# Attention followed by two gated MLPs on one core: the second batch's query side is issued between the first gate products

## Chip, cores and metric

One NeuronCore of a Trainium2 chip runs the whole program. The metric is the device time of one execution in microseconds (us). The kernel before took 1736.15 us (median of 3 runs, 1733.27 to 1736.31).

## What is computed

Eight batches of eight heads, 576 positions, head width 64. A pack of 32 queries per head first attends to keys and values; the queries `q` then attend to the 32 packed rows. The result, 4608 tokens of 512 values, is scaled by its root mean square and goes through a gated MLP (512 to 1536 to 512, SiLU) and a second one (512 to 2048 to 512).

```python
p_packed = sm_attn(p, k, v)                 # softmax over 576 keys
out      = sm_attn(q, p_packed, p_packed)   # softmax over 32 packed rows
x   = out as (4608, 512)
xn  = x / sqrt(mean(x*x) + 1e-6) * rms_g
h   = (silu(xn @ w_gate) * (xn @ w_val)) @ w_out
u   = h @ w_in
res = (u * sigmoid(1.702 * u)) @ w_out2
```

## The kernel before

**Chains.** `attention` (L121) works on chains: chain n is one half of a batch's heads (four heads; NG = 2 halves per batch, so chains 0 and 1 are batch 0, chains 2 and 3 batch 1). Two batches make a unit; there are four units. A chain has two sides.

- The packed side: load k, p, v (L156), transposes of k and p on TensorE (`heads_t` L263 and `p_t` L247), first scores `s1` (L274 on TensorE, maxima L284 to L289 on VectorE, exponentials L293 on ScalarE), transposes of the exponentials `a_t` (L307), product with v `pv` (L319), transposes of that `pp_t` (L340), which also writes the weights' left side `Lh`, `Ll` (L349 to L351).
- The query side: load q (`load_q`), ten transposes `heads_t(n, "q", ...)` (L263), second scores `s2` (two groups of columns, 256 and 320; L274), then in a row: transposes to `t` on VectorE (L359), maxima (L364), subtraction on GpSimd (L365), exponentials on ScalarE (L366), sums (L368 to L371), multiplication on GpSimd (L372), `weights`, a transpose into the tile `AT` on VectorE (L378), products `x` (L396) whose squares are summed on ScalarE (L401, tile `jk`). When both halves of a batch are squared, the mean square and its power follow (L408, L409 on VectorE, L411 on GpSimd) and `scale` (L414) multiplies `AT` by it (matmul L422, product L431). `scaled` (L634) then splits `AT` into `Aqh` and `Aql` (L642, L643), which the gate products read.

**The first MLP.** `run` (in `mlp1`) goes through steps; step s is 128 columns of the gate and value weights. `prods` (L610) makes the step's stationary tiles `Wh`, `Wl` (matmul L628, L630, L631). `gateval(s, o)` (L644, matmul L659, o the batch within the unit) makes gate and value; `project` (L679) multiplies by `w_out`. The weights arrive as packed words and are converted piece by piece: `piece` (L573) runs `convert` (L102: ScalarE L108, VectorE L109 to L112, ScalarE L113, GpSimd L114) and then fetches the next raw piece (L570) into one of two `raw` buffers, so that a fetch waits for the conversion of the piece two before.

**What sets the order.** For unit 0 `start` (L433) writes a list of calls, each with a number (a position, not a measured time), sorted by it. Calls below LEADING = 38 are issued first, with conversions between them (L982 to L987). The rest is given out while `run` issues the first gate products: one call per EVERY/len(todo) estimated TensorE ns (L992, L1018). When `run` yields "attention" (after step 1 of batch 0), all that is left is issued, then `scaled(0, 1)` and the gate products of batch 1. A scheduler at build time then settles each engine's order; the engines run their instructions in that order. The query tiles and, from chain 4 on, the key tiles share one tag `kq` with two buffers in pool `at`; all loads go through the SP queue.

```python
while todo[0][0] < LEADING:
    time, calls = todo.pop(0)
    act(calls)
    while time > spent:
        piece()
        spent += PACE
```

Of the kernel before, what the change touches and what calls it, by code (L numbers as in the profile page):

```python
# [28 lines left out]
def tile_pack_attention__then__two_mlps(  # L29
# [32 lines left out]
    NG = H * NP // P  # L62
# [56 lines left out]
    chains = [(b, g) for b in range(B) for g in range(NG)]  # L119

    def attention(at, first, lp, psum, getL, getAT):  # L121
# [311 lines left out]
        def start(period, after):  # L433


            todo = []

            def do(time, *calls):
                todo.append((time, len(todo), calls))

            for n in range(LEAD):
                t0 = period * n
                do(t0 - 50 if n < 2 else t0 - 2 * period + 2.6, (load_kp, n))
                do(t0 - 30 if n < 1 else t0 - period + 2.5, (load_v, n))
                do(t0 - 29 if n < 1 else t0 - period + (3.5, 14)[n > 1], (load_q, n))
                do(t0 + 1.2, (p_mask, n), (p_t, n))
                for i in range(4):
                    do(t0 + 0.5 * i, (heads_t, n, "k", i // 2, i % 2))
                do(t0 + 3.5, (s1, n, 0))
                do(t0 + 4.2, (s1, n, 1))  # L450
                do(t0 + 3.0, (split_v, n))
                do(t0 + 8, (a_t, n, 0))
                do(t0 + 8.6, (a_t, n, 1))
                do(t0 + 11, (pv, n))
                do(t0 + 14.5, (pp_t, n))
                for i in range(4):
                    do(t0 + 11.2 + 0.5 * i, (heads_t, n, "q", i // 2, i % 2))
                do(t0 + 17, (s2, n, 0))
                do(t0 + 17.7, (s2, n, 1))
                do(t0 + 23, (weights, n))  # L460
                for i in range(-(-NC // 2)):
                    do(t0 + 25 + 0.6 * i, (x, n, 2 * i))
                if n % NG == NG - 1:
                    for e in range(2):
                        do(t0 + 30 + 0.6 * e, (scale, chains[n][0], e))
            t0 = period * LEAD
            do(t0 + 2, (load_kp, after))
            do(t0 + 14, (load_v, after))
            do(t0 + 15, (load_q, after))
            do(t0 + 20, (p_mask, after), (p_t, after))  # L470
            for i in range(4):
                do(t0 + 23.1 + 0.5 * i, (heads_t, after, "k", i // 2, i % 2))
            return [(t, calls) for t, _, calls in sorted(todo, key=lambda x: x[:2])]

        def stages(seq, after, whole):
# [52 lines left out]
            return todo  # L528

        return start, stages  # L530


# [541 lines left out]
```

## Time and profile before

| what | value |
|---|---|
| runs | 1733.27, 1736.31, 1736.15 us |
| profiled execution | 1733.05 us, its span 1731.3 us |
| TensorE matmul (PE) | 1690.9 us, 98% of the span |
| VectorE (DVE) | 896.6 us, 52% |
| ScalarE (ACT) | 683.1 us, 39% |
| GpSimd (POOL) | 497.1 us, 29% |
| granted TensorE clock, mean | 0.997 |

Busy times are means over stages with different limits: VectorE is busy for 88% of the stretch from 100 to 300 us, far more than over the whole span. A chain that decides something is read from the timeline of its engines, and a wait from the row of the instruction that waits.

### The profile page before, as it was taken

The page shows a single profiled execution, that of the slowest core. Times are in us where ns is not written, and L with a number is a line of the kernel's source. Part 1 is how long each engine was busy: PE and PEld are TensorE (multiplying, and loading weights), DVE is VectorE, ACT ScalarE, POOL GpSimd, SP SyncE. Part 2 cuts the span into 40 slices and gives each one's busy share as a digit, 9 for nine tenths or more (in the row PEclk, how much of TensorE's full clock was granted, in tenths as well). Part 3 has the DMA queues.
Part 4 walks back from the last instruction along what each step waited for, and adds up shares of the span by engine and source line. Part 5 has one row for each costly group of instructions (what it writes and reads, how often), then busy time and mean ns, then how long its engine had stood idle before and what let it go on. Part 6 is the DMA issues. An engine that isn't in the chain of part 4 may idle for free.

```text
span 1731.3 us, 24694 instructions
## 1 busy us (share of the span) xinstructions
PE 1690.9 (98%) x9400; PEld 1497.7 (87%) x9400; DVE 896.6 (52%) x1792; ACT 683.1 (39%) x1511; POOL 497.1 (29%) x479
## 2 busy tenths in 40 slices
PE   7899999999999999999999999999999999999998
PEld 5699898999999999999988888888888888888887
DVE  6888898557666576678884742222222222122221
ACT  5676676655555555555553321111111111111111
POOL 2446777544554354445643200000000000000000
PEclk9999999999999999999999999999999999999999
DMA  9556656544425442356656410101010101000000
GB/s 263 153 168 196 194 177 198 176 139 145 125 88 172 142 143 97 105 206 235 235 192 226 145 58 1 49 0 49 1 49 0 49 0 49 0 21 4 18 8 25
DMA packets 152343, 186.16 MB, mean 108 GB/s; under 512 B 87073, under 2 KB 123937, under 8 KB 145185
## 3 DMA queue, kind: packets, MB, share of 16 engines
q1 hardware_dynamic: 152224, 184.58, 33.4%
q8 instruction: 74, 1.21, 0.3%
q14 instruction: 45, 0.36, 0.1%
HBM read 139.46 MB, written 45.09 MB: 107 GB/s over the span
## 4 chain that ended last, share of the span: by engine, by line
PE 86%; DVE 5%; DMA 3%; ACT 3%; issue 1%; POOL 1%; SPq 1%; ACTq 0%; POOLq 0%; DVEq 0%
PE ps_dn L885 23%; PE ps_up L866 23%; PE ps_o L690 15%; PE ps_g L659 15%; PE ps_w L628 3%; PE ps_at L274 2%; PE ps_at L319 2%; PE ps_at L263 2%; PE ps_at L396 1%; DMA raw<-in_moe_w_in_dram 1%; DMA raw<-in_moe_w_out_dram 1%; DVE Wl L631 1%; DMA raw<-in_moe_w_val_dram 1%; SPq L156 1%; ACT Wh L630 1%
## 5 line engine op out<-in xcount | busy, mean ns | idle before, releaser
L866 PE MATMUL ps_up<-xh,wi 128*128 128x512 f32 x1152 | 381.8, 393 | 2.4 <-issue 1.6
L885 PE MATMUL ps_dn<-wo,gh 128*128 128x512 f32 x1152 | 356.4, 391 | 0.0
L690 PE MATMUL ps_o<-Hh,wo 128*128 128x384 f32 x1152 | 325.5, 341 | 4.2 <-ACT add L703 2.9
L872 DVE CAST gh<-gf 128x512 fp32r<-128x512 f32 x144 | 63.3, 440 | 509.0 <-ACT gf L869 508.9
L869 ACT ACTIVATE gf<-ps_up 128x512 f32<-128x512 f32 x144 | 86.2, 599 | 609.7 <-PE ps_up L866 588.6
L866 PEld LDWEIGHTS ps_up<-xh,wi 128*128 128x128 f32 x1152 | 216.2, 188 | 52.1 <-POOL wo L114 2.0
L885 PEld LDWEIGHTS ps_dn<-wo,gh 128*128 128x128 f32 x1152 | 216.3, 188 | 47.5
L659 PE MATMUL ps_g<-Aqh,Wh 128*128 128x288 f32 x768 | 235.4, 307 | 11.4 <-DVE th L667 4.1
L659 PE MATMUL ps_g<-Aqh,Wl 128*128 128x288 f32 x768 | 226.6, 296 | 0.6 <-DVE Wl L631 0.6
L659 PE MATMUL ps_g<-Aql,Wh 128*128 128x288 f32 x768 | 227.0, 296 | 0.0
L866 PE MATMUL ps_up<-xl,wi 128*128 128x512 f32 x576 | 225.8, 392 | 0.0
L885 PE MATMUL ps_dn<-wo,gl 128*128 128x512 f32 x576 | 224.4, 391 | 0.0
L690 PEld LDWEIGHTS ps_o<-Hh,wo 128*128 128x128 f32 x1152 | 209.9, 188 | 8.7 <-ACT add L703 4.0
L690 PE MATMUL ps_o<-Hl,wo 128*128 128x384 f32 x576 | 193.3, 337 | 0.8 <-POOL Hl L676 0.8
L676 POOL TENSOR_TENSOR Hl<-th,Hh 128x576 fp32r<-128x576 f32 x96 | 137.8, 1436 | 176.3 <-ACT Hh L675 174.3
L631 DVE TENSOR_TENSOR Wl<-ps_w,Wh 64x512 fp32r<-64x512 f32 x192 | 131.7, 687 | 80.6 <-ACT Wh L630 77.6
L659 PEld LDWEIGHTS ps_g<-Aqh,Wh 128*128 128x128 f32 x768 | 144.8, 189 | 17.7 <-DVE th L667 5.5
L705 POOL TENSOR_TENSOR acc<-acc,add 128x384 f32<-128x384 f32 x135 | 136.3, 1021 | 68.8 <-ACT add L703 67.0
L659 PEld LDWEIGHTS ps_g<-Aqh,Wl 128*128 128x128 f32 x768 | 144.5, 188 | 1.2 <-DVE Wl L631 0.8
L659 PEld LDWEIGHTS ps_g<-Aql,Wh 128*128 128x128 f32 x768 | 145.1, 189 | 0.0
L630 ACT CAST Wh<-ps_w 64x512 fp32r<-64x512 f32 x192 | 111.5, 581 | 79.1 <-PE ps_w L628 47.7
L885 PEld LDWEIGHTS ps_dn<-wo,gl 128*128 128x128 f32 x576 | 108.1, 188 | 24.7
(150 smaller groups left out, 2527.7 us busy)
## 6 DMA issues: line engine op xcount, KB each, us to landing
wg<-wg SPq DMA_DIRECT2D x48, 1024.0 KB, 5.4
wo<-wo SPq DMA_DIRECT2D x48, 512.0 KB, 4.1
raw<-in_moe_w_out_dram SPq DMA_DIRECT2D x28, 512.0 KB, 3.6
x<-acc SPq DMA_DIRECT2D x32, 288.0 KB, 2.7
out_dram<-ob SPq DMA_DIRECT2D x36, 256.0 KB, 2.0
vn<-in_v_dram SPq DMA_DIRECT2D x16, 512.0 KB, 6.3
qn<-in_q_dram SPq DMA_DIRECT2D x64, 128.0 KB, 5.0
raw<-in_moe_w_in_dram SPq DMA_DIRECT2D x16, 512.0 KB, 3.9
```

What stands on the lines that cost most here:

```text
L263: nc.tensor.transpose(ps[:, o : o + size(c)], src[: size(c), c, 2 * a : 2 * a + 2, :].rearrange("p h d -> p (h d)"), ident[: size(c), : si ...
L628: nc.tensor.matmul(ps[:, a], st[:, i], mv[:, i], start=n == 0, stop=n == 2)
L630: nc.scalar.copy(Wh[rows, :, g], src)
L631: nc.vector.tensor_sub(Wl[rows, :, g], src, fl(Wh[rows, :, g]))
L659: nc.tensor.matmul(ps, st[:, o, g, c * P : (c + 1) * P], mv[:, g, cols], start=n == 0, stop=n == 3 * NG - 1)
L676: nc.gpsimd.tensor_sub(Hl, th, fl(Hh))
L690: nc.tensor.matmul(ps, st[:, m * P : (m + 1) * P], mv[:, cols], start=n == 0, stop=n == 3 * len(ss) - 1)
L705: nc.gpsimd.tensor_add(a, a, t)
L866: nc.tensor.matmul(ps, st[:, i], mv[:, i], start=n == 0, stop=n == 3 * NM - 1)
L869: nc.scalar.activation(gf, ps, AF.Gelu_apprx_sigmoid)
L872: nc.vector.tensor_copy(gh, gf)
L885: nc.tensor.matmul(pacc[r], st[:, r * P : (r + 1) * P], mv, start=f == 0 and n == 0, stop=f == NF2 - 1 and n == 2,)
```

## The change

In `start`, the query side of chains 2 and 3 (batch 1 of unit 0: `heads_t` "q", `s2`, `weights`, `x`, `scale`) gets 24 added to its numbers, so that all of it lies above LEADING. It is issued in the second part of the list, between the first gate products. The calls for chain 4 (the next unit's first: `load_kp`, `load_v`, `load_q`, `p_mask`, `p_t`, `heads_t` "k") get new numbers too. The second part has 30 entries in place of 19.

```diff
             for n in range(LEAD):
                 t0 = period * n
+                late = 24 if n >= NG else 0
...
                 for i in range(4):
-                    do(t0 + 11.2 + 0.5 * i, (heads_t, n, "q", i // 2, i % 2))
-                do(t0 + 17, (s2, n, 0))
-                do(t0 + 17.7, (s2, n, 1))
-                do(t0 + 23, (weights, n))
+                    do(late + t0 + 11.2 + 0.5 * i, (heads_t, n, "q", i // 2, i % 2))
+                do(late + t0 + 17, (s2, n, 0))
+                do(late + t0 + 17.7, (s2, n, 1))
+                do(late + t0 + 23, (weights, n))
                 for i in range(-(-NC // 2)):
-                    do(t0 + 25 + 0.6 * i, (x, n, 2 * i))
+                    do(late + t0 + 25 + 0.6 * i, (x, n, 2 * i))
                 if n % NG == NG - 1:
                     for e in range(2):
-                        do(t0 + 30 + 0.6 * e, (scale, chains[n][0], e))
+                        do(late + t0 + 30 + 0.6 * e, (scale, chains[n][0], e))
             t0 = period * LEAD
-            do(t0 + 2, (load_kp, after))
-            do(t0 + 14, (load_v, after))
-            do(t0 + 15, (load_q, after))
-            do(t0 + 20, (p_mask, after), (p_t, after))
+            do(t0 + 24, (load_kp, after))
+            do(t0 + 25, (load_v, after))
+            do(t0 + 31, (load_q, after))
+            do(t0 + 32, (p_mask, after), (p_t, after))
             for i in range(4):
-                do(t0 + 23.1 + 0.5 * i, (heads_t, after, "k", i // 2, i % 2))
+                do(t0 + 34 + 0.5 * i, (heads_t, after, "k", i // 2, i % 2))
```

No instruction is added or removed. Lines below L443 are one higher in the changed kernel (L659 there is L660). Three places of the new order follow; `ps_at`, `ps_g` and `ps_w` are accumulator banks, the numbers behind names are tile numbers.

**Place 1.** TensorE at chain 3's first scores (`kTh_504`, `pTh_539`); `AT00` is chain 0's tile, `vn_287` chain 2's values. Before:

```order
L274 MATMUL ps_at_553<-qTh_453,kept_451 128x256 x2
L274 MATMUL ps_at_558<-kTh_504,pTh_539 128x256 x2
L274 MATMUL ps_at_612<-kTh_504,pTh_539 128x320 x2
L396 MATMUL ps_at_626<-pph_310,AT00_139 128x256 x2
L263 MATMUL ps_at_633<-ident_99,qn_486 128x128 x2
L263 MATMUL ps_at_633<-ident_99,qn_486 128x64
```

Now:

```order
L274 MATMUL ps_at_553<-qTh_453,kept_451 128x256 x2
L274 MATMUL ps_at_558<-kTh_504,pTh_539 128x256 x2
L396 MATMUL ps_at_621<-pph_310,AT00_139 128x256 x2
L396 MATMUL ps_at_628<-pph_310,AT00_139 64x256
L274 MATMUL ps_at_576<-qTh_453,kept_451 128x320 x2
L396 MATMUL ps_at_592<-pph_310,AT00_139 128x256 x2
L319 MATMUL ps_at_599<-vn_287,aTh_525 128x256 x5
L274 MATMUL ps_at_607<-kTh_504,pTh_539 128x320 x2
```

The second half of chain 3's first scores (128x320) moved behind chain 0's products, chain 1's second scores and chain 2's product with v.

**Place 2.** ScalarE around the last squares of batch 0 (`jk` with `ss_590`); `w<-raw` is the first step of a conversion, which needs a piece fetched from memory. Before:

```order
L401 ACTIVATE jk_744,ss_590<-ps_at_741 128x256
L135 COPY qTh_736<-ps_at_748 128x320
L401 ACTIVATE jk_746,ss_590<-ps_at_741 128x256
L135 COPY qTh_736<-ps_at_762 128x256
L113 CAST wg_771<-w_772 128x4x128
L135 COPY qTh_736<-ps_at_766 128x320
L135 COPY kept_734<-ps_at_783 128x256
L401 ACTIVATE jk_755,ss_590<-ps_at_753 64x256
```

Now:

```order
L113 CAST wo_660<-w_661 128x512
L113 CAST wg_716<-w_717 128x4x128
L108 ACTIVATE w_898<-raw_670 128x512
L401 ACTIVATE jk_692,ss_590<-ps_at_689 128x256
L108 ACTIVATE w_1053<-raw_726 128x512
L401 ACTIVATE jk_694,ss_590<-ps_at_689 128x256
L135 COPY kept_687<-ps_at_705 128x256
L401 ACTIVATE jk_698,ss_590<-ps_at_696 64x256
L643 CAST Aqh_786<-AT00_139 128x576
```

Two conversions' first steps moved in front of the last three squares of batch 0. On the SP queue the fetch of `raw_726` moved to the place right behind that of `raw_670`, ahead of chain 4's loads.

**Place 3.** TensorE ahead of batch 1's scale (`ri_1045` now, `ri_974` before); `AT10` and `AT11` are the tiles of chains 2 and 3, `Aqh_786` and `Aqh_853` batch 0's. Before, chain 3's second scores and its products stand among the first products of the MLP:

```order
L274 MATMUL ps_at_823<-qTh_736,kept_734 128x256 x2
L274 MATMUL ps_at_839<-qTh_736,kept_734 128x320 x2
L396 MATMUL ps_at_871<-kept_605,AT10_141 128x256 x2
L396 MATMUL ps_at_878<-kept_605,AT10_141 128x256 x2
L396 MATMUL ps_at_898<-kept_605,AT10_141 64x256
L422 MATMUL ps_at_794<-ident_99,ri_760 128x128 x2
L422 MATMUL ps_at_800<-ident_99,ri_760 128x128 x2
```

Now:

```order
L660 MATMUL ps_g_1064<-Aqh_786,Wl_820 128x288
L396 MATMUL ps_at_967<-kept_605,AT10_141 128x256 x2
L263 MATMUL ps_at_984<-ident_99,kn_802 128x128 x2
L263 MATMUL ps_at_989<-ident_99,kn_802 128x128 x2
L263 MATMUL ps_at_989<-ident_99,kn_802 128x64
L396 MATMUL ps_at_995<-kept_605,AT10_141 128x256 x2
L396 MATMUL ps_at_1010<-kept_605,AT10_141 64x256
L396 MATMUL ps_at_1015<-kept_687,AT11_142 128x256 x2
L396 MATMUL ps_at_1031<-kept_687,AT11_142 128x256 x2
L396 MATMUL ps_at_1038<-kept_687,AT11_142 64x256
L422 MATMUL ps_at_1047<-ident_99,ri_1045 128x128 x2
```

Chain 2's and chain 3's products moved from around batch 0's scale (`ri_760`) to a place behind the last gate product of batch 0 (`ps_g_1064`), directly ahead of batch 1's scale.

## Rows read from the trace of the kernel before

**Rows 1.** The page, part 1: busy time and share of the span.

```profile
PE 1690.9 (98%) x9400; PEld 1497.7 (87%) x9400; DVE 896.6 (52%) x1792; ACT 683.1 (39%) x1511; POOL 497.1 (29%) x479
```

**Rows 2.** Windows: stretch, length, busy us (instructions) of PE, PEld, DVE, ACT, POOL, clock, DMA.

```profile
42.80:91.76 48.96, 42.30 (x218) 31.92 (x217) 40.96 (x82) 31.82 (x94) 21.66 (x26) 0.97 0.53 158
100.00:300.00 200.00, 192.23 (x1302) 181.93 (x1301) 175.39 (x363) 139.90 (x325) 136.36 (x131) 1.00 0.62 190
```

**Rows 3.** Waits of PE, 42.8 to 91.8 us: total us, times, longest us.

```profile
PE ps_g L659 <- ACT Wh L630: 3.7, 2, 3.2
PE ps_at L274 <- ACT kept L135: 2.2, 2, 1.6
```

**Rows 4.** Timeline of PE: start us, us, engine, line, out<-in, xcount [idle before <-releaser].

```profile
41.75 2.14 PE L274 MATMUL ps_at<-kTh,pTh 128*128 128x256 f32 x8
43.73 1.03 PE L396 MATMUL ps_at<-pph,AT 128*128 128x256 f32 x4
...
47.15 2.52 PE L319 MATMUL ps_at<-vn,aTh 128*128 128x256 f32 x10
...
52.97 2.21 PE L274 MATMUL ps_at<-qTh,kept 128*128 128x256 f32 x8 [0.66 <-ACT kept L135]
...
60.14 1.43 PE L263 MATMUL ps_at<-ident,qn 128*128 128x128 f32 x8
...
63.50 2.21 PE L274 MATMUL ps_at<-qTh,kept 128*128 128x256 f32 x8 [1.56 <-ACT kept L135]
...
68.17 1.52 PE L422 MATMUL ps_at<-ident,ri 128*128 128x128 f32 x10
...
74.57 0.40 PE L659 MATMUL ps_g<-Aqh,Wh 128*128 128x288 f32 x1 [3.25 <-ACT Wh L630]
...
85.00 0.60 PE L422 MATMUL ps_at<-ident,ri 128*128 128x128 f32 x4
...
91.76 0.37 PE L659 MATMUL ps_g<-Aqh,Wh 128*128 128x288 f32 x1
...
96.02 0.29 PE L659 MATMUL ps_g<-Aqh,Wh 128*128 128x288 f32 x1
...
97.48 0.29 PE L659 MATMUL ps_g<-Aqh,Wl 128*128 128x288 f32 x1
```

**Rows 5.** Timeline of ACT (ScalarE), same columns.

```profile
46.86 0.48 ACT L293 ACTIVATE e<-ps_at,nm 128x256 f32<-128x256 f32 x1
...
59.49 0.70 ACT L108 ACTIVATE w<-raw 128x512 f32<-128x512 f32 x1 [2.34 <-DMA raw<-in_moe_w_val_dram]
...
63.29 0.39 ACT L401 ACTIVATE jk<-ps_at 64x256 f32<-64x256 f32 x1
...
80.74 0.38 ACT L401 ACTIVATE jk<-ps_at 64x256 f32<-64x256 f32 x1
```

**Rows 6.** Timeline of the SP queue: issue of transfers, same columns.

```profile
55.70 0.38 SPq L570 DMA_DIRECT2D raw<-in_moe_w_val_dram  x1
...
65.42 4.07 SPq L156 DMA_DIRECT2D qn<-in_q_dram  x5
```

**Rows 7.** Timelines of DVE (VectorE) and POOL (GpSimd), same columns.

```profile
53.35 0.69 DVE L111 SCALAR_TENSOR_TENSOR between<-raw,between 128x512 int32<-128x512 int32 x1
53.94 0.77 DVE L378 STREAM_TRANSPOSE AT<-t 128x576 f32<-128x576 f32 x1
...
64.79 0.77 DVE L378 STREAM_TRANSPOSE AT<-t 128x576 f32<-128x576 f32 x1
...
74.52 0.78 DVE L378 STREAM_TRANSPOSE AT<-t 128x576 f32<-128x576 f32 x1 [0.45 <-POOL t L372]
...
65.76 1.18 POOL L411 TENSOR_TENSOR ri<-ms,mhalf 128x5 f32<-128x5 f32 x1 [0.40 <-DVE ms L409]
...
83.50 1.17 POOL L411 TENSOR_TENSOR ri<-ms,mhalf 128x5 f32<-128x5 f32 x1
```

**Rows 8.** Windows, columns as in rows 2.

```profile
76.00:77.00 1.00, 1.00 (x5) 0.82 (x4) 0.97 (x3) 0.44 (x1) 0.00 (x0) 0.50 0.00 0
```

## The prediction, made before the changed kernel ran

> **What bounds the kernel now.** The page's first part comes first: TensorE is busy for 1690.9 us, 98% of the span [rows 1], so whatever this change gives or takes must show as TensorE waiting less or more; the work itself stays. The windows tell where waiting is left. From 42.8 us, where the two orders first differ on TensorE, to 91.76 us, where batch 1's first gate product starts, TensorE is busy 42.30 of 48.96 us, so it waits 6.7 us; from 100 to 300 us it waits another 7.8 (200 less 192.23) [rows 2]. The list of waits names the first stretch's: 3.7 us for `Wh` and 2.2 us for `kept`, both ScalarE's [rows 3]. The timelines then give the chain: chain 3's second scores end at 65.7 (63.50 and 2.21), batch 0's scale starts at 68.17, the first gate product at 74.57 after a wait of 3.25, batch 1's scale at 85.00, batch 1's first product at 91.76 [rows 4]. So before, the 26 us that chain 3 needs from its second scores to batch 1's first product lie beside other TensorE work.
>
> **What the change moves.** It adds and removes nothing. Behind batch 0's scale now stand, of batch 1's two chains, twenty transposes, both second scores and both products. The best it can bring is that batch 0's scale comes much sooner. I follow three stretches to batch 1's first gate product; up to 42.7 us all is as before.
>
> *First stretch, to batch 0's scale.* Place 1: chain 3's first scores now wait for work put ahead of them. In the old rows the eight matmuls of one score pair take 1.98 us (41.75 to 43.73), so 0.9 for 256 columns and 1.1 for 320; a `x` pair 0.86, its 64-row rest 0.43, a `pv` 2.45 (from its row's start to the next instruction's) [rows 4]. From 42.7: 0.86, 0.43, 1.1, 0.86, 2.45, 1.1 gives 49.5. From there to the first exponential passed 3.1 us before (43.73 to 46.86 [rows 4, 5]); in the new order fewer conversion steps stand between on VectorE, so I take 2.6, and 1.0 for the two exponentials: 53.1. VectorE then has `r1`, its reciprocal (0.2 each), one transpose to `AT` (0.70) and eight conversion steps at 0.6 (53.35 to 53.94 is one [rows 7]): 5.9 us, so the second of two raw buffers is free at 59.0.
>
> Place 2 decides what follows. The piece fetched into that buffer (`raw_726`) is needed by a ScalarE instruction that stands ahead of the last two squares of batch 0. A fetch took 3.79 us from issue to its first use: issued at 55.70, used at 59.49, with ScalarE idle for 2.34 before it [rows 5, 6]. So that instruction starts at 62.8 and the squares behind it end 1.7 us later (0.6, then three short ones), at 64.5. From the last square's start to the end of the power took 3.65 us once (63.29 to 66.94) and 3.93 once (80.74 to 84.67) [rows 5, 7], and from its own end, 0.5 later, 3.2 and 3.4; a handover to TensorE is 0.2. That is 64.5 + 3.2 + 0.2: batch 0's scale starts at about 67.9, not sooner than the 68.17 of before. TensorE, done with `pv` and its transposes at about 60, stands for 8 us. The Trainium skill, "DMA: Bandwidth & Descriptors", section "Anatomy of one DMA — SWDGE (gpsimd) path", fits a transfer as 2.0 us plus bytes over 436,000 per us; that is an estimate of 3.2 us for these 512 KB, for another issuing path, and would put the scale 0.6 earlier; the trace's 3.79 is used.
>
> *Second stretch, to the end of chain 3's second scores.* TensorE's own work, in the new order: the scale 1.45; 24 products for `Wh` and 33 gate products at no more than 0.133 each (twelve in 96.02 to 97.48) 7.6; 27 transposes at 0.17 (eight took 1.36 from 60.14) 4.6; two second scores 4.0 [rows 4]. That is 17.6, and the chains beside it are shorter than that in parts, so I take no wait: 85.5. The loads of chain 4's q wait now for chain 3's transposes in this stretch: they took 4.07 us of the SP queue [rows 6], and the next raw piece stands behind them, so ScalarE may be held until about 87.6 once more; by then VectorE still has a backlog of its own, and I charge nothing.
>
> *Third stretch, to batch 1's first product.* Place 3: only 15 gate products (2.0), chain 2's products (2.2) and some transposes are left to cover chain 3's softmax. From the end of second scores to the transpose into `AT` it took 9.6 us for chain 2 (55.18 to 64.79) and 8.8 for chain 3 (65.71 to 74.52). I take 11, since VectorE and GpSimd now have gate steps and conversions between these steps. From `AT` to the scale it took 10.5 (74.52 to 85.00), with its products at half clock; I take 7.2 (0.7 transpose, 2.2 products, 1.0 for the last squares, 3.3 to the power). From scale to first product it took 6.8 (85.00 to 91.76) and 6.4 (68.17 to 74.57) [rows 4, 7]; now only the scale itself and the next unit's first scores stand there, so 3.4 (1.45, twelve at 0.13, two transposes). Together 21.6, with bounds 8.8 + 7.2 + 3.4 = 19.4 and 11 + 10.5 + 6.8 = 28.3. Batch 1's first product starts at about 107.1.
>
> *The sum.* 107.1 less 91.76 is 15.3; in it TensorE has done 2.0 us (those twelve scores, two transposes) that stood behind before, so the delay is 13. From there the order is much as before. VectorE is some steps ahead after waiting so long, and part of the 7.8 us of later waits [rows 2] may shrink; I give back 2. That is +11 on an execution of 1733.05 us, whose span is 1731.3. The median of the three runs shown is 3.1 above that execution, and on it the forecast is 1736.15 + 11, rounded to **1747**.
>
> **Rivals.** *Half clock.* After the wait of 3.25 us the clock was 0.50, the 1.2 GHz level, at 76 to 77 us [rows 8], and batch 1's products ran slow. My walk has five waits of 2.5 us or more (near 50, 60, 88, 93 and 98 us). If four cost 1.5 us each, as that one did, and lie on the path: 13 + 6 - 2, +17, 1753. The Trainium skill, "TensorE: Matmul & The Clock Gate", section "HAM oscillation — how this bites in real kernels", has the clock drop again after each such wait. Against it: in these stretches other engines set the time, so slow matmuls hide. 0.12.
>
> *All given back.* The later 7.8 us of waits vanish because the other engines are ahead: 13 - 7.8, about +5, 1741. For it: those waits are for products of other engines. Against it: buffers hold only two pieces, so no engine gets far ahead. 0.13.
>
> *Nothing left.* The third stretch at its lower bound (19.4) with all waits given back: +3, 1739. 0.11.
>
> *Faster: VectorE is the real bound.* Place: 42.8 to 300 us, where VectorE is busy for 40.96 of 48.96 and 175.39 of 200 us [rows 2]. If its stream sets the end of this stretch, moving work to where it stood idle saves up to the 8.0 us of the first window: -8, 1728. It decides if VectorE has done all that precedes batch 1's first product before 91.76. Against it: TensorE is at 96% from 100 to 300 us and VectorE at 88%, and by the walk VectorE waits too. 0.06.
>
> That the change might not do what it says is ruled out by the three places.
>
> **How the numbers follow.** The forecast case (+7 to +16) has 0.58. What a measurement of this kernel tells from no change is 0.2%, 3.5 us. Slower by more holds the forecast, half clock and all given back: 0.58 + 0.12 + 0.13 = 0.83. Same is "nothing left", 0.11; faster 0.06. The range runs from 1737, which leaves out the faster case and a third of "nothing left", to 1756, which leaves out the worst of half clock with both bounds together: some 0.15 outside.
>
> **What would show it.** Right: batch 0's scale at 66.5 to 69 us after a TensorE wait of 6 us or more; ahead of it a ScalarE L108 with an idle time ended by a raw transfer; chain 3's second scores ending near 85; waits of 2 us or more before chain 2's products, chain 3's products and batch 1's scale; batch 1's first product at 103 to 110. The window from 42.8 us to that product would hold 20 us of TensorE idle. The prediction is wrong if batch 0's scale comes before 64, if batch 1's first product comes before 97, or if the waits from there to 300 us shrink by more than 5 us.

## The result and the profile after

The changed kernel takes **1756.4 us** (median of four runs, 1751.04 to 1756.7) beside 1735.74 for the kernel before: ratio 1.0119, 95% interval 1.0104 to 1.0134. The direction was right; the size was not: +20.7 us where the forecast was +11, and 0.4 us above the range's upper end. A second set of runs of the same kernel, below, gave 1754.75, inside the range: the range was missed narrowly, the forecast by nearly as much as it was. The profiled execution is the fastest of the four (1751.04), 18.0 us over that of before. Its busy times, page part 1:

```profile
PE 1696.5 (97%) x9400; PEld 1502.3 (86%) x9400; DVE 893.3 (51%) x1792; ACT 683.6 (39%) x1511; POOL 496.3 (28%) x479
```

The same instructions run [rows 1]; TensorE's busy time even grew by 5.6 us, since slow matmuls count as busy. The windows (columns as in rows 2), of the kernel before:

```profile
42.80:115.00 72.20, 65.55 (x376) 54.32 (x375) 61.37 (x130) 47.97 (x132) 33.11 (x37) 0.98 0.54 161
115.00:320.00 205.00, 197.23 (x1334) 186.96 (x1333) 174.94 (x361) 141.64 (x330) 140.48 (x134) 1.00 0.61 187
```

and after:

```profile
42.80:115.00 72.20, 53.34 (x234) 40.40 (x233) 44.77 (x91) 35.19 (x97) 24.91 (x30) 0.81 0.42 125
115.00:320.00 205.00, 197.60 (x1346) 187.83 (x1346) 175.82 (x376) 141.83 (x332) 136.31 (x130) 1.00 0.61 186
```

By these windows all of the loss lies before 115 us. There TensorE stands 18.9 us instead of 6.7, and the granted clock falls from 0.98 to 0.81. From 115 to 320 us it stands 7.4 us, 7.8 before: nearly nothing is given back. The waits of TensorE after, 42.8 to 114.9 us (total, times, longest), beside [rows 3]:

```profile
PE ps_at L422 <- POOL ri L411: 11.7, 2, 6.4
PE ps_at L396 <- DVE AT L378: 3.0, 2, 2.4
PE ps_at L307 <- ACT e L293: 2.3, 1, 2.3
PE ps_g L660 <- DVE Wl L632: 1.7, 1, 1.7
```

The waits for `Wh` and `kept` are gone; those for both scales' `ri` and for `AT` have come. TensorE's timeline after, the places of [rows 4]:

```profile
49.00 1.34 PE L274 MATMUL ps_at<-kTh,pTh 128*128 128x320 f32 x4
...
69.40 2.69 PE L422 MATMUL ps_at<-ident,ri 128*128 128x128 f32 x10 [6.43 <-POOL ri L411]
...
87.29 1.24 PE L274 MATMUL ps_at<-qTh,kept 128*128 128x320 f32 x4
...
94.94 2.07 PE L396 MATMUL ps_at<-kept,AT 128*128 128x256 f32 x4 [2.36 <-DVE AT L378]
...
98.10 5.62 PE L396 MATMUL ps_at<-kept,AT 128*128 128x256 f32 x16
...
109.01 2.69 PE L422 MATMUL ps_at<-ident,ri 128*128 128x128 f32 x10 [5.29 <-POOL ri L411]
...
114.85 0.78 PE L660 MATMUL ps_g<-Aqh,Wh 128*128 128x288 f32 x4
```

Batch 0's scale stands at 69.40 (forecast 67.9), chain 3's second scores end at 88.53 (85.5), batch 1's first gate product starts at 114.85 (107.1). So the walk is 1.5 us short in its first stretch, 1.5 in its second and 4.7 in its third. Why, two views show. ScalarE and the SP queue, first stretch [rows 5, 6]:

```profile
61.69 0.66 ACT L108 ACTIVATE w<-raw 128x512 f32<-128x512 f32 x1 [1.88 <-DMA raw<-in_moe_w_val_dram]
65.56 0.66 ACT L108 ACTIVATE w<-raw 128x512 f32<-128x512 f32 x1 [2.84 <-DMA raw<-in_moe_w_gate_dram]
...
66.73 0.38 ACT L401 ACTIVATE jk<-ps_at 64x256 f32<-64x256 f32 x1
...
91.59 0.68 ACT L108 ACTIVATE w<-raw 128x512 f32<-128x512 f32 x1 [2.27 <-DMA raw<-in_moe_w_val_dram]
...
57.91 0.38 SPq L571 DMA_DIRECT2D raw<-in_moe_w_val_dram  x1
59.64 0.38 SPq L571 DMA_DIRECT2D raw<-in_moe_w_gate_dram  x1
```

Two raw pieces are fetched 1.73 us apart. The first takes 3.78 us to its use, the second 5.92, and the squares stand behind both. The windows of three slow stretches, and of the one ahead of the second:

```profile
69.00:74.00 5.00, 4.60 (x20) 4.24 (x20) 2.23 (x5) 1.30 (x3) 0.64 (x2) 0.52 0.01 3
...
88.00:95.00 7.00, 2.90 (x18) 2.12 (x17) 6.91 (x14) 2.93 (x7) 3.58 (x3) 0.95 0.59 219
95.00:101.00 6.00, 6.00 (x15) 3.65 (x15) 4.33 (x9) 4.20 (x12) 3.75 (x3) 0.50 0.45 127
...
109.00:114.80 5.80, 5.79 (x23) 5.41 (x24) 3.47 (x8) 1.24 (x2) 0.00 (x0) 0.50 0.00 0
```

The slow ones have a granted clock of 0.50 or 0.52, so matmuls at 1.2 GHz: behind the waits of 6.43 and 5.29 us, and behind seven us in which TensorE was busy for 2.90. The scale took 2.69 us where it took 1.52 [rows 4], and the way from batch 1's scale to its first product 5.84 us where I took 3.4. The Trainium skill, "TensorE: Matmul & The Clock Gate", section "HAM oscillation — how this bites in real kernels", tells of waits between bursts of matmuls that bring the low clock back each time; the trace agrees for the waits of 6.43 and 5.29 us. The third stretch stands behind work in pieces. What the low clock costs in the end is another question (below).

### The profile page after: what moved, and what is told of

It is laid out like the page before. It is cut to its first block, busy times and chain, and to the rows that moved or that the text cites. A ratio compares the mean times of both kernels' runs of the same rounds, so it can differ in the third digit from the quotient of the medians.

```text
span 1749.3 us, 24687 instructions
## 1 busy us (share of the span) xinstructions
PE 1696.5 (97%) x9400; PEld 1502.3 (86%) x9400; DVE 893.3 (51%) x1792; ACT 683.6 (39%) x1511; POOL 496.3 (28%) x479
## 4 chain that ended last, share of the span: by engine, by line
PE 83%; DVE 5%; DMA 5%; ACT 2%; POOL 2%; issue 2%; SPq 1%; ACTq 0%; POOLq 0%; DVEq 0%
PE ps_dn L886 23%; PE ps_up L867 22%; PE ps_o L691 14%; PE ps_g L660 13%; PE ps_w L629 3%; PE ps_at L274 2%; PE ps_at L263 2%; PE ps_at L319 2%; PE ps_at L396 1%; DMA vn<-in_v_dram 1%; DMA raw<-in_moe_w_in_dram 1%; DVE Wl L632 1%; DMA raw<-in_moe_w_out_dram 1%; DMA raw<-in_moe_w_val_dram 1%; SPq L156 1%
## 5 line engine op out<-in xcount | busy, mean ns | idle before, releaser
L660 PE MATMUL ps_g<-Aqh,Wh 128*128 128x288 f32 x768 | 233.6, 305 | 8.8 <-DVE th L668 5.1
L660 PE MATMUL ps_g<-Aqh,Wl 128*128 128x288 f32 x768 | 226.2, 296 | 1.7 <-DVE Wl L632 1.7
L660 PE MATMUL ps_g<-Aql,Wh 128*128 128x288 f32 x768 | 226.4, 295 | 0.0
L660 PEld LDWEIGHTS ps_g<-Aqh,Wh 128*128 128x128 f32 x768 | 144.2, 188 | 14.5 <-DVE th L668 7.0
L660 PEld LDWEIGHTS ps_g<-Aqh,Wl 128*128 128x128 f32 x768 | 144.1, 188 | 2.2 <-DVE Wl L632 2.0
L660 PEld LDWEIGHTS ps_g<-Aql,Wh 128*128 128x128 f32 x768 | 144.5, 188 | 0.0
L631 ACT CAST Wh<-ps_w 64x512 fp32r<-64x512 f32 x192 | 111.5, 581 | 78.1 <-PE ps_w L629 50.5
```

Of the source, the lines that this page charges most:

```text
L631: nc.scalar.copy(Wh[rows, :, g], src)
L660: nc.tensor.matmul(ps, st[:, o, g, c * P : (c + 1) * P], mv[:, g, cols], start=n == 0, stop=n == 3 * NG - 1)
```

## The experiments

Three theories. **Uncovered way**: what must happen between chain 3's second scores and batch 1's first product has lost the TensorE work that stood beside it, so the loss goes as soon as enough of batch 0's products stand there again. (Experiment 2 refutes this form; what took its place was read from the traces afterwards.) **Holds**: ScalarE waits for raw pieces, and GpSimd for chain 4's values, ahead of the squares and powers that the scales need. **Half clock**: the slow matmuls are on the path. Rounds of the kernel before ran beside each; "ratio" is to those.

**1. Half of the change** (also the rival that chain 4's later loads cost).

```
- late = 24 if n >= NG else 0
+ late = 0
```

> Half of the change undone: chains 2 and 3 stand where they stood before (`late` is 0 for all), chain 4's loads and key transposes keep their later numbers. Theory (the loss comes from batch 1's query side, which now stands uncovered behind batch 0's scale): the time is that of the kernel before within 3 us, 1734 to 1739, and batch 1's first gate product starts at 91 to 94 us. Rival (the loads of chain 4 behind the other loads, or the SP queue, cost the time): most of the 18 to 20 us stays, 1750 or more.

1732.48 us, ratio 0.9985 (0.9972 to 0.9998); batch 1's first product at 89.37. Run once more:

> The kernel with chain 4's numbers alone once more, with five rounds, since its first result (ratio 0.9985, interval 0.9972 to 0.9998) lies near no change. If the gain is real: 1730 to 1734, 2 to 4 us under the kernel before. If not: within 1.5 us of it.

1732.14 us, 0.9988 (0.9976 to 1.0001). Chain 4's numbers cost nothing and may gain 2 us, less than the 0.2% that I call telling. The loss comes with the delay of chains 2 and 3; that delay without chain 4's new numbers was not run. The changed kernel itself, once more:

> The changed kernel once more, unaltered, to have its time and a second trace beside the kernels that share its runs of the kernel before. Expected: 1751 to 1757; in the trace the same order of waits (batch 0's scale after 6 us or more of TensorE waiting for `ri`, batch 1's first product at 113 to 118 us).

1754.75 us, 1.0109 (1.0096 to 1.0123); scale at 70.75 after 6.94 us, first product at 115.67. Two values then stand for the changed kernel, 1756.4 and 1754.75.

**2. How far the delay goes**: `late = 4`, `late = 8`, and 24 for chain 3 alone (`if n == NG + 1`).

> The delay given to batch 1's queries' side cut from 24 to 4 steps of the table: chain 3's second scores now stand among the products for `Wh` around batch 0's scale, all of batch 0's gate products behind them. Theory (the loss is chain 3's uncovered way from its second scores to batch 1's first gate product; it goes as soon as about 14 us of batch 0's products stand beside that way): no wait over 2 us for batch 1's products and scale, batch 1's first product at 88 to 93 us, time 1730 to 1738, like the kernel with chain 4's numbers alone. Rival (the first-scale wait, caused by the raw pieces ahead of batch 0's squares, is the larger part, and it stays with any delay): 1742 or more.

1745.87 us, 1.0064 (1.005 to 1.0077): a miss. TensorE, with 4:

```profile
70.89 0.70 PE L274 MATMUL ps_at<-qTh,kept 128*128 128x320 f32 x2
...
93.38 2.69 PE L422 MATMUL ps_at<-ident,ri 128*128 128x128 f32 x10 [3.33 <-POOL ri L411]
...
98.66 1.33 PE L660 MATMUL ps_g<-Aqh,Wh 128*128 128x288 f32 x4
```

The wait at batch 0's scale is only 0.24 us here and batch 0's products all stand beside the way, yet batch 1's product starts 6.9 us later than before. So neither the theory nor the reason given for its rival holds.

> The same with 8 steps. By the theory of the uncovered way each further step that chain 3's second scores move behind gate products takes cover away: with about 10 us of products left beside a way of 20 to 26 us it should lie between the 4-step and the 24-step kernel, 1736 to 1746, with the waits at batch 1's products and scale larger than with 4 steps. Rival (a threshold: all or nothing): within 2 us of either.

1754.15 us, 1.0115 (1.01 to 1.013): a miss too, already the whole loss, as the rival (all or nothing) had it.

> The 24 steps for chain 3 alone (the later half of batch 1); chain 2's second scores, product and transposes stand where they stood before. Theory (it is the last chain's way that sets batch 1's scale, so chain 2 may stand anywhere): most of the loss stays, 1746 to 1756, with the waits before chain 3's products and batch 1's scale together 6 us or more. Rival (both chains' softmax and conversions crowd the other engines, so half the chains cost half): 1740 to 1745.

1750.78 us, 1.0094 (1.0078 to 1.0109), with 8.61 us of waiting for chain 3's `AT` and 4.56 for its `ri`: as expected, chain 3 alone makes most of the loss. The table has the end of chain 3's second scores (start plus length of its last row), the start of batch 1's first product, the time between them, and the time from that product to the end of the span:

```
                      second scores end   first product   between   to the end
before                      65.71             91.76         26.0      1639.5
chain 4's numbers alone     65.91             89.37         23.5      1638.4
the same, again             66.37             89.81         23.4      1639.1
late = 4                    71.59             98.66         27.1      1641.8
late = 8                    81.61            107.72         26.1      1642.8
24, chain 3 alone           84.32            110.45         26.1      1636.5
changed                     88.53            114.85         26.3      1634.5
changed, again              89.64            115.67         26.0      1637.9
```

That is the main finding: in the five executions with a delay the way is 26 to 27 us long, with few or with all of batch 0's products beside it, and in each of them TensorE stands for `ri` ahead of batch 1's scale (3.33, 4.08, 4.56, 5.29 and 5.29 us). There the way is the path, so each us by which chain 3's second scores start later comes out at the first product. This was read from the traces after both expectations had missed; no run was made to test it alone.

That the kernel before has 26.0 as well is in part luck. TensorE worked through nearly all of that time; its waits in it are 3.25 and 0.42 us for `Wh` and 0.63 for `Wl`, none for `AT` or `ri`, and from the scale to the first product it had 6.8 us of work to do. With chain 4's numbers alone, where less stands there, it is 3.88 us, and the way is 23.5:

```profile
85.49 1.41 PE L422 MATMUL ps_at<-ident,ri 128*128 128x128 f32 x10
...
89.37 1.06 PE L660 MATMUL ps_g<-Aqh,Wh 128*128 128x288 f32 x4 [1.07 <-ACT Aqh L643]
```

Nor does the end follow the first product one for one: with 8 it starts 7.1 us sooner than in the changed kernel, and that execution ended 1.3 us later (spans of 1750.5 and 1749.3 us). The changed kernel had 2 us of TensorE work (twelve scores) in front of the product which stand behind it with 8. Beyond that, the last column's spread of 8.3 us is not explained here.

**3. Half clock: filling the waits.** The identity is multiplied by itself ahead of the scale, into the bank which the scale overwrites.

```
+ if e == 0 and b < 2:
+     for _ in range(24):
+         nc.tensor.matmul(ps[:, :P], ident, ident, start=True, stop=True)
```

> The changed kernel with 24 matmuls of the identity by itself (128 columns each) ahead of each of the first two scales, into the scale's own PSUM bank, which the scale then overwrites. They only fill the time in which TensorE waits for `ri`. Theory (half clock after the long waits costs time, against my prediction's sentence that slow matmuls hide): the matmuls behind both scales run at 0.13 us in place of 0.21 to 0.27, the stretch from batch 1's scale to its first product falls from 5.8 to about 3.5 us, that from batch 0's scale to the end of chain 3's second scores from 19 to about 17.5, and the time falls by 3 to 5 us, to 1751 to 1753 beside 1756. Rival (slow matmuls hide behind other engines): the stretches and the time stay, within 1.5 us.

1755.42 us, 1.0114 (1.0099 to 1.0129): no gain beside 1756.4 and 1754.75. Locally it did what was expected, the scale in 1.52 us and batch 1's first product 3.27 us behind its start in place of 5.84:

```profile
111.89 1.52 PE L426 MATMUL ps_at<-ident,ri 128*128 128x128 f32 x10 [0.15 <-POOL ri L412]
...
115.16 0.78 PE L664 MATMUL ps_g<-Aqh,Wh 128*128 128x288 f32 x4
```

and its window behind:

```profile
115.00:320.00 205.00, 195.05 (x1314) 183.72 (x1313) 173.67 (x366) 139.24 (x330) 133.35 (x128) 1.00 0.60 183
```

There TensorE stands 9.95 us in place of 7.4 (7.86 in the changed kernel's second execution); that what was won at the scale is waited for later fits this and is not shown by it. This execution was also 2.7 us behind by the end of chain 3's first scores (53.04 for 50.34), ahead of the first filling, so its places are read from there. My sentence "slow matmuls hide" fails for the way from batch 1's scale to its first product and holds, as far as this run tells, for the end.

**4. Holds.** `keep_in_program_order` keeps an instruction from being moved ahead of program order; here the `L108` of the two pieces of place 2 (`pin` is `n in (7, 8)`).

```
- nc.scalar.activation(wf, top.bitcast(F32), AF.Abs)
+ i = nc.scalar.activation(wf, top.bitcast(F32), AF.Abs)
+ if pin:
+     tc.keep_in_program_order(i)
```

> The changed kernel with the two conversion instructions that wait for raw pieces (`raw_670`, `raw_726`) held in program order on ScalarE, so that they stand behind batch 0's squares. Theory (ScalarE stands at these two while the squares behind them are ready; this sets batch 0's scale): the scale starts at 64 to 66 in place of 69.4, the wait before it falls from 6.4 to 2 to 3 us, and of the 4 to 5 us at least 2 are left at the end: 1751 to 1754 beside 1756. Rival (the power is ready no sooner because VectorE or GpSimd are late, or what is won at the first scale is waited for at chain 3's products): the scale comes no more than 1 us sooner, or the time stays within 1.5 us.

1750.61 us, 1.009 (1.0075 to 1.0105), 4 to 6 us less. The last square and batch 0's scale:

```profile
64.48 0.38 ACT L403 ACTIVATE jk<-ps_at 64x256 f32<-64x256 f32 x1
...
67.14 2.07 PE L424 MATMUL ps_at<-ident,ri 128*128 128x128 f32 x10 [2.97 <-POOL ri L413]
```

The wait fell from 6.43 to 2.97 us; the hold at 91.59 is gone too, and the way is 24.2 us long (88.43 to 112.66). The first hold I had priced 2 us too low, the later one at nothing. With both edits:

> Both: squares ahead of the two waiting conversions, and 24 identity matmuls ahead of each of the first two scales. If both causes act by themselves their gains add: 5 to 9 us less than the changed kernel, 1747 to 1751. If the path behind the first scale is set by chain 3's softmax on the other engines, the first gain goes into the wait before chain 3's products (2.4 us and more) and the time is that of the matmuls alone, 1751 to 1753. If neither is on the path: 1755 to 1757.

1751.55 us, 1.0095 (1.0076 to 1.0114), but the fillings outlasted the shorter waits (`ri` was ready at 66.38, the scale started at 68.66), so this run parts nothing. Chain 4's value split alone, its two instructions held likewise inside `split`:

```
- split([vh[part], vl[part]], vn[part], nc.gpsimd)
+ split([vh[part], vl[part]], vn[part], nc.gpsimd, n == LEAD)
```

> The changed kernel with chain 4's value split alone held in program order (no raw piece held). If the 3 us of GpSimd ahead of batch 1's power and the 1.4 us between are on the path: 1751 to 1753, 3 to 4 us less than the changed kernel. If they are covered and the raw pieces were all: 1754 to 1757.

1759.08 us, 1.0138 (1.0123 to 1.0153): the first product came 3.3 us sooner than in the changed kernel's second run (112.36), the way was 22.4 us long (from 89.93), and the time grew: neither expectation. Window behind:

```profile
115.00:320.00 205.00, 195.54 (x1303) 185.30 (x1303) 175.12 (x364) 140.55 (x329) 138.05 (x132) 0.98 0.60 183
```

TensorE stands 2.1 us longer there than in the changed kernel, and a clock of 0.98 in place of 1.00 is worth some 4 us of 205 (an estimate). That the split now stands in the way of later steps is argued, not shown. Three pieces and the split together (the edit above and this):

```
- convert(cv, raw.pop(n), parts, DM, mm)
+ convert(cv, raw.pop(n), parts, DM, mm, n in (7, 8, 9))
```

> The changed kernel with three conversion instructions that wait for raw pieces (numbers 7, 8, 9) and the splitting of chain 4's values (vh, vl) held in program order, so that ScalarE's squares and GpSimd's power of both batches have neither ahead of them. In the trace of the kernel with two pieces held, ScalarE's third raw wait was gone as well, and 3 us of GpSimd's `vl` stood ahead of batch 1's power. Theory (what my sum left out are these waits of other engines for transfers and for chain 4's values): 2 to 4 us less than the kernel with two held, 1747 to 1749; from batch 1's last square to its scale 3 us in place of 4. Rival (those 3 us are covered or only move to the next wait): 1750 to 1752.

1746.64 us, 1.0073 (1.0053 to 1.0093), 8 to 10 us less than the changed kernel. TensorE:

```profile
84.94 1.24 PE L279 MATMUL ps_at<-qTh,kept 128*128 128x320 f32 x4
...
102.12 1.52 PE L427 MATMUL ps_at<-ident,ri 128*128 128x128 f32 x10 [0.97 <-POOL ri L416]
...
105.40 0.77 PE L665 MATMUL ps_g<-Aqh,Wh 128*128 128x288 f32 x4
```

Here the way is 19.2 us long: 9.0 to the transpose into `AT` (at 95.14), 7.0 to the scale, 3.3 to the product. I had taken 11, 7.2 and 3.4, together 2.4 us more. The time is +12, about my forecast; this is another kernel than the one forecast. With a filling on top:

> As the kernel before this one, with 24 identity matmuls ahead of each of the first two scales. With holds, value split and half clock gone, what remains is the uncovered way of chain 3 (11 us in my prediction's sum). If the miss was these three: 1745 to 1748, +10 to +13 to the kernel before. If half clock costs nothing at the end, as the kernel with the identity matmuls alone suggested: the same as without them, within 1.5 us.

1757.74 us, 1.0133 (1.0113 to 1.0152): neither expectation. The reason is the experiment's own:

```profile
99.09 6.32 PE L428 MATMUL ps_at<-ident 128*128 128x128 f32 x48
105.24 0.61 PE L431 MATMUL ps_at<-ident,ri 128*128 128x128 f32 x4
...
100.28 1.18 POOL L417 TENSOR_TENSOR ri<-ms,mhalf 128x5 f32<-128x5 f32 x1
```

`ri` was ready at 101.46 and the scale came 3.8 us later, behind its filling (24 matmuls, two rows of the trace each). With 12 and 4 in place of 24 each:

> As the kernel with three raw pieces and the value split held, with 12 identity matmuls ahead of batch 0's scale and 4 ahead of batch 1's (some 2.8 and 0.9 us, in place of 24 each, which took 5.5 to 6.3 us there and outlasted the waits). If half clock costs at the end: 1742 to 1745, 2 to 4 us less than the 1746.6 without them. If slow matmuls hide: 1745 to 1748.

1744.78 us, 1.006 (1.0041 to 1.0079), first product at 103.88. 1.9 us less than without, inside the first expectation's 1742 to 1745, but the two intervals overlap: a gain of some 2 us from the clock is possible here and not shown.

**5. Is there a better kernel?** Chain 4's value load left at 14, in the kernel of 1:

```
- do(t0 + 25, (load_v, after))
+ do(t0 + 14, (load_v, after))
```

> Chain 4's numbers alone, but its value load left where it stood before (14 instead of 25). In the trace of the former, ScalarE stood 3.39 us at a cast of chain 4's values (`vh`), which waited for the late transfer, and a wait of TensorE for a tanh behind it took 1.28 us. If that hold costs: 1 to 2 us less than the kernel with all of chain 4's numbers. If it is covered: the same within 1 us. If chain 4's value split, now back among batch 0's steps, is what slowed the kernel before: 2 to 4 us more, like the kernel before.

1738.01 us, 1.0015 (1.0003 to 1.0027), 5.9 more than with 25, above all three expectations. The other way round, 25 in place of 14 in the kernel before:

> The kernel before with one number altered: chain 4's value load at 25 instead of 14. With all of chain 4's numbers the time was 1732.1 to 1732.5, with all but the value load's 1738.0. If the value load alone makes the difference: 1730 to 1734. If it needs the others with it: 1734 to 1738.

1733.96 us, 0.9992 (0.9982 to 1.0002): the one number alone makes no difference that can be told. And three held pieces (7, 8, 9) in the kernel of 1:

> Chain 4's numbers alone (no late queries) with three raw pieces held in program order, so that no raw wait stands ahead of batch 0's squares on ScalarE. In that kernel's trace ScalarE stood 2.27 us for a raw piece at 59.70, and TensorE waited 1.97 us for Wh at 73.48. If the hold is on the path there too: 1729 to 1731, 1 to 3 us less than chain 4's numbers alone. If the products beside it cover it: the same within 1 us.

1746.68 us, 1.006 (1.0046 to 1.0074), 14 more: neither expectation. Both scales came sooner (66.81 and 82.13, for 68.37 and 85.49), and then

```profile
96.03 0.69 PE L249 MATMUL ps_at<-ident,pbm 128*128 128x128 f32 x2 [8.91 <-POOL pbm L241]
...
97.67 1.04 ACT L137 CAST vh<-vn 128x1024 fp32r<-128x1024 f32 x1 [10.06 <-DMA vn<-in_v_dram]
```

The next raw fetch (84.30 for 81.31) and chain 4's loads behind it in the SP queue (86.70 for 83.78) come 3 us later. TensorE's wait for `pbm`, 8.91 us, is 0.35 us with chain 4's numbers alone. That TensorE had nothing left to cover them, because the earlier scales had pulled its other work forward, is argued and was not tried. A like edit gained 4 to 6 us in one order and lost 14 in another. No kernel here beats the one before by more than 0.2%.

## Why the prediction was wrong in size

- *Direction and place*: right, and the mechanism in the main: TensorE stands where its work was taken away, and the other engines' steps set the time. Batch 0's scale is no sooner (69.40 for 68.17) after a wait of 6.43, with the two raw waits of ScalarE ahead of it; waits of 2.36 and 5.29 us stand before chain 2's products and batch 1's scale; TensorE idles 18.9 us where I said 20. The times that I named all came late: 69.40 for "66.5 to 69", 88.53 for "near 85", 114.85 for "103 to 110". A wait of 2 us or more before chain 3's products did not come: they follow chain 2's, slow, in one run of rows.
- *First stretch*, 1.5 us short: the term "a fetch took 3.79 us". It was taken from a fetch by itself; `raw_726` went out 1.73 us behind another and took 5.92. About 1 us of this came back: from the last square's start to the power's end it was 2.62 us (66.73 to 69.35) where I had seen 3.65 and 3.93, and the handover to TensorE, 0.2 in my sum without a row, was 0.05. The Trainium skill's fit ("DMA: Bandwidth & Descriptors", section "Anatomy of one DMA — SWDGE (gpsimd) path"), an estimate of 3.2 us for another issuing path, was lower than either.
- *Second stretch*, 1.5 us short: I took every matmul at full clock; it ran at 0.52 from 69 to 74 us.
- *Third stretch*, **the step that failed most**: "together 21.6", measured 26.3, inside my bounds of 19.4 and 28.3. To the transpose into `AT` it was 11.45 us (88.53 to 99.98) for my 11; two other terms were too small. *From `AT` to the scale* I took 7.2, and it was 9.0: chain 4's value split (`vl`) stood ahead of the power on GpSimd, and VectorE's two small steps beside it were long. The kernel before has both, in rows that I left out:

```profile
80.18 3.09 POOL L137 TENSOR_TENSOR vl<-vn,vh 128x1024 fp32r<-128x1024 f32 x2 [5.70 <-ACT jk L401]
...
81.24 1.35 DVE L408 TENSOR_TENSOR ms<-ss 128x5 f32<-128x5 f32 x1 [0.39 <-ACT jk L401]
```

I shortened its 10.5 us as if this would go, and it stayed. *From the scale to the first product* I took 3.4, and it was 5.84. That was right as to the work (3.88 with chain 4's numbers alone, 3.28 with the holds gone) and wrong in "slow matmuls hide": here they ran at half clock on the path. In the changed kernel, GpSimd and VectorE ahead of batch 1's scale:

```profile
103.86 3.01 POOL L137 TENSOR_TENSOR vl<-vn,vh 128x1024 fp32r<-128x1024 f32 x2 [3.91 <-ACT jk L401]
106.83 0.71 POOL L239 TENSOR_TENSOR pbm<-pb,mask 128x256 f32<-128x256 f32 x1
107.78 1.18 POOL L411 TENSOR_TENSOR ri<-ms,mhalf 128x5 f32<-128x5 f32 x1
...
99.98 0.78 DVE L378 STREAM_TRANSPOSE AT<-t 128x576 f32<-128x576 f32 x1 [0.82 <-POOL t L372]
...
105.45 0.77 DVE L408 TENSOR_TENSOR ms<-ss 128x5 f32<-128x5 f32 x1 [4.69 <-ACT jk L401]
106.25 0.70 DVE L409 TENSOR_SCALAR ms<-ms 128x5 f32<-128x5 f32 x1
```

- *"I charge nothing"* for ScalarE's later hold: it was there (2.27 us at 91.59). Taken away together with the first one, it belongs to the 4 to 6 us of the held pieces; its own share was not measured.
- *Given back*: 3 us of 21.1 between the first product and the end, forecast 2 of 13. With the spread of the table's last column this is no more than agreement in kind.
- *Rivals*: half clock came about as a mechanism (its four slow stretches, the fourth from 55 to 61 us with a granted clock of 0.57) but not as the end's price: filling the waits changed the time by 1 us or less alone, by 1.9 with the holds gone. The three others, which had less or none of the delay left at the end, did not come.

Shown is that the loss comes with the delay, that in the delayed kernels the first product follows chain 3's second scores at 26 to 27 us, and that this way grows shorter when holds are taken out of it: 24.2 us with two pieces held, 22.4 with the split alone, 19.2 with three pieces and the split. Open is how the 8 to 10 us at the end divide: held pieces alone give 4 to 6, the split alone loses, and together they give most.

## What to carry to other kernels

When the same two events stand before and after a move, set the distance between them as the old trace has it, whole, beside the sum of its shortened parts, and name for each part shortened what the move takes away. Here, with my own 85.5 for the second scores, the whole distance gives 111.5 for the first product in place of my 107.1, and with the measured 88.53 it gives 114.6 (measured 114.85). That it comes so close is in part luck: in the old kernel TensorE's own work filled it, in the new one waits and slow matmuls. And look at what is queued ahead of the small steps of such a way on the engines that are "off the path": a conversion that waits for a transfer, a 3 us split ahead of a 1 us power.

## What the runs showed that was not expected

- Two 512 KB fetches issued 1.73 us apart came into use 3.87 us apart (61.69 and 65.56), about as long as the 3.79 us from issue to use of one that was issued by itself [rows 5, 6]: the second got little from having been issued early. A transfer of `wo` was issued 0.48 us behind it; which of the two slowed it, if either, is not shown.
- VectorE's two instructions on 128x5 numbers ahead of the power took 0.77 and 0.70 us while GpSimd worked on `vl`; in the kernel with the split held, where GpSimd stood, they took 0.17 each:

```profile
100.38 0.17 DVE L413 TENSOR_TENSOR ms<-ss 128x5 f32<-128x5 f32 x1 [4.46 <-ACT jk L406]
100.58 0.17 DVE L414 TENSOR_SCALAR ms<-ms 128x5 f32<-128x5 f32 x1
```

- Filling a wait with matmuls brought the clock to 1.00 in both stretches behind the scales, and bought nothing at the end; where the filling was longer than the wait, it cost its excess and more (1757.74 beside 1746.64).
